# Fetch two pairs ahead, fillers thinned, the last store on another queue: a fused attention and token-routing kernel

## The chip, the cores and the metric

The kernel runs on one NeuronCore of a Trainium2 chip. The core has a matmul engine (PE; weight loads are listed apart as PEld), a vector engine (DVE), a scalar engine (ACT), GpSimd (POOL), SyncE (SP), which here only issues transfers, and 16 DMA engines. Time is device microseconds of one execution; the kernel before takes 159.84 us, median of 3 runs (159.52 to 160.04). A span is the part of it that the profile covers.

## The reference

Two parts follow each other. Attention in chunks of 32 queries: each sees 56 keys (16 to the left, its own 32, 8 to the right) and 8 memory keys. Then a routed FFN: per batch the 128 best of 768 tokens by a gate score get an FFN added.

```python
for c in range(768 // 32):                  # batch 4, 8 heads, head_dim 64
    k_full = concat(mem_k, k[max(0, 32*c-16) : min(768, 32*c+40)])
    a = softmax(q[32*c : 32*c+32] @ k_full.T / 8)
    out[32*c : 32*c+32] = a @ v_full
x = out as [4, 768, 512]                    # heads side by side
scores = x @ w_gate                         # [4, 768]
for b in range(4):
    top = argpartition(-scores[b], 128)[:128]
    xe = x[b, top]
    ye = relu(xe @ w1) @ w2                 # 512 -> 1024 -> 512
    out[b, top] = xe + sigmoid(scores[b, top])[:, None] * ye
```

## The kernel before

Work goes in 16 pairs of heads, n = 0 to 15, four to a batch. Everything is written out in program order for each engine; nothing reorders it later. One turn of the main loop (L537) handles three pairs at once: scores of pair n+1, values of pair n, transposes of pair n+2. It has eight places: scores n+1 first half, q transposes, values n first half ("value half n,0"), k transposes, scores second half, back transposes of the windowed v (vw to vc), value half n,1, v transposes. Between them `hook(i)` calls the steps of the routed FFN that a table puts there (L474 to L500): step i of batch b runs at place i mod 8 of pair 4(b+1) + i div 8. So batch b's routing and FFN run beside the attention of the batches after it; those of batch 2 end, and those of batch 3 run, behind the loop (L576 to L599).

The steps are: six dots with the gate vector on DVE (`m_dot`), transposes that put the scores in a row (`m_row`), a sigmoid (`m_gate_exp`, `m_gate`), six comparisons of all pairs of scores (`m_cmp`) whose matmul counts give each token's rank (`m_count`), a mask and a slot number (`m_mask`, `m_slot`), one-hot selections (`m_sel`), index and gate by a matmul with them and then the indirect DMA that fetches the chosen rows from the output in DRAM (`m_aux` and `m_fetch`, L406), transposes of these rows (`m_rows`, L413), two halves of the first FFN layer (`m_ffn1`), and the second layer with a scatter that adds to the output (`m_ffn2`). Batch 3 does not fetch: it gathers from SBUF by matmuls (`m_gather`).

Transfers go out on two queues. GpSimd issues all loads (converting fp32 to fp16), the fetches and the scatters; SyncE issues the gate vector and the stores of x (`m_store`, two transfers a batch). Loads go by units of two pairs with four buffers, so a unit is issued when the one four before it has been used. Fillers (`fill`, `fill_into`) are matmuls of zeros whose result nobody reads. PSUM pools that the fillers use: pmm (one bank, all routing steps), pxx (one bank, values), pss (two banks, scores and batch 3).

Of the kernel before, what the change touches and what calls it, by code (L numbers as in the profile page):

```python
# [8 lines left out]
FP = mybir.dt.float32  # L9
# [8 lines left out]
def _dap(x, offset, dims):  # L18
    return bass.AP(tensor=x.tensor, offset=offset, ap=[list(d) for d in dims])
# [7 lines left out]
def kernel(  # L27
# [13 lines left out]
    nc = tc.nc  # L41
    B, H, S, D = q.shape
    n_mem = mem_k.shape[2]
    cap = int(moe_capacity)
    Dm = H * D
# [5 lines left out]
    NB = 6  # L51
# [11 lines left out]
    pxx = ctx.enter_context(tc.tile_pool(name="pxx", bufs=1, space=bass.MemoryType.PSUM))  # L63
# [50 lines left out]
    def fill_into(ap, n=1):  # L114
        for _ in range(n):
            nc.tensor.matmul(out=ap, lhsT=zeros[:, 0:128], rhs=zeros, start=True, stop=True)  # L116

    def fill(n):
        fill_into(pmm.tile([128, 1, 512], FP, tag="pm", name="p_f")[:, 0, :], n)

    p_t = ptt.tile([128, 8, 100], F16, tag="tp", name="p_t")
    pads = p_t.bitcast(FP)
# [90 lines left out]
    def tr_q(n):  # L213
        if n >= NPR:
            return
        p_q = pvv.tile([128, 8, 128], F16, tag="pv", name="p_q")[:, :, 0:96]
        transposes(q16s, n, p_q)
        qT = att.tile([128, 96, 8], F16, tag="qT", name="qT")
        nc.scalar.copy(out=qT, in_=p_q.rearrange("p j t -> p t j"))  # L219
        qTs[n] = qT  # L220

    def mem_cols(t, src, n):
        eng = nc.vector if n < 4 else nc.gpsimd
        eng.tensor_copy(out=t.rearrange("p g (j t) -> p g j t", t=16)[:, :, :, 15],  # L224
                              in_=src[:, :, n].unsqueeze(1).to_broadcast([128, NG, n_mem]))

    def tr_k(n):
        if n >= NPR:
            return
        transposes(k16s, n)  # L230
        kw = kws[n % SLOTS]
        nc.vector.tensor_copy(out=kw.rearrange("p g (j t) -> p g j t", t=16),  # L232
                              in_=_sap(p_t, 0, [[12, NG], [100, 8], [1, 16]]))
        if n:
            mem_cols(kw, memkT, n)
# [20 lines left out]
    def scores(n, half, fills=0):  # L256
        if n >= NPR:
            return
        kw, qT = kws[n % SLOTS], qTs[n]
        qf = qT.rearrange("p t j -> p (t j)")  # L260
        p_s = pss.tile([128, 2, 512], FP, tag="ps", name="p_s")
        fill_into(p_s[:, 0, :], fills)
        for gi, g in enumerate(GROUPS[half]):
            for h in range(2):
                o = 64 * h
                nc.tensor.matmul(out=p_s[:, h, 96 * gi:96 * gi + 96], lhsT=kw[o:o + 64, g, :],  # L266
                                 rhs=qf[o:o + 64, 96 * g:96 * g + 96], start=True, stop=True)
        es = att.tile([128, 2, 4, 96], F16, tag="es", name="es")
        pv = p_s[:, :, 0:384].rearrange("p s (g t) -> p s g t", t=96)
        for c in range(3):  # L270
            nc.scalar.activation(out=es[:, :, :, 32 * c:32 * c + 32], in_=pv[:, :, :, 32 * c:32 * c + 32],  # L271
                                 func=AF.Exp, bias=maskb[:, c:c + 1], scale=0.125)
        ess[n, half] = es
# [40 lines left out]

    def m_store(b):
        x = xs[b]
        nc.sync.dma_start(out=_dap(out, b * S * Dm, [[Dm, 96], [96 * Dm, NB], [1, Dm]]), in_=x[0:96, :, :])
        nc.sync.dma_start(out=_dap(out, (b * S + 576) * Dm, [[Dm, 32], [32 * Dm, NB], [1, Dm]]), in_=x[96:128, :, :])

    def m_alloc(b):  # L320
        m = mods[b]
# [145 lines left out]
    def moe_steps(b):  # L467

        st = {}

        def at(i, f, *a):
            st.setdefault(i, []).append(lambda: f(b, *a))

        at(0, m_alloc)  # L474
        p = dict(dots=(0, 3, 6, 7, 8, 11), row0=12, row1=15, gate=17, cmps=(18, 19, 22, 23, 24, 27),
                 counts=(22, 23, 26, 27, 28, 31), mask=32, slot=34, sel=35, fetch=38, rows=45, ffn=(47, 49, 51))
        if b == LAST - 2:
            p.update(fetch=37, rows=43, ffn=(45, 46, 47))
        if b == LAST - 1:
            p = dict(dots=(0, 1, 3, 4, 6, 7), row0=9, row1=11, gate=12, cmps=(13, 14, 15, 17, 18, 19),  # L480
                     counts=(16, 17, 18, 20, 21, 22), mask=22, slot=24, sel=24, fetch=26)
        for i in range(NB):
            at(p["dots"][i], m_dot, (i,))
        at(p["row0"], m_row, 0, 4)
        at(p["row1"], m_row, 4, 6)
        at(p["row1"], m_gate_exp)
        at(p["gate"], m_gate)
        for i in range(NB):
            at(p["cmps"][i], m_cmp, (i,))
        for i in range(NB):  # L490
            at(p["counts"][i], m_count, (i,))
        at(p["mask"], m_mask)
        at(p["slot"], m_slot)
        at(p["sel"], m_sel)
        at(p["fetch"], m_fetch)
        if b < LAST - 1:
            at(p["rows"], m_rows)
            at(p["ffn"][0], m_ffn1, 0)
            at(p["ffn"][1], m_ffn1, 1)
            at(p["ffn"][2], m_ffn2)  # L500
        return st
# [8 lines left out]
        for f in places.get(i, ()):  # L510
            f()

    fill(8)
    tr_k(0)
    fill(2)
    tr_q(0)
# [1 line left out]
    mem_cols(kws[0], memkT, 0)  # L518
    fill(2)
    tr_v(0)  # L520
    fill(1)
    scores(0, 0)
    mem_rows(memv16, memvT)
    for n in range(3):
        mem_cols(vws[n], memvT, n)
    tr_k(1)
    fill(2)
    scores(0, 1)
    tr_q(1)
    fill(2)  # L530
    back_v(0)
    tr_v(1)
    fill(1)
    late_constants()
    scrA = mod.tile([128, NB], FP, tag="scrA", name="scrA")
    scrB = mod.tile([128, NB], FP, tag="scrB", name="scrB")
    for n in range(NPR):  # L537
        b, pr = divmod(n, NP)
        i = 8 * n
        nf = 1  # L540
        if b >= 1 and pr == 0:
            m_store(b - 1)
        if n == 1:
            nc.sync.dma_start(out=wgb, in_=_dap(moe_w_gate, 0, [[0, 128], [1, Dm]]))
        if n == NPR - 2:
            m_alloc(LAST)
        scores(n + 1, 0, nf if b == 0 else 0)
        hook(i)
        if n == NPR - 1:
            m_dot(LAST, range(NB), 0, 2, scrA)  # L550
        if 3 <= n + 3 < NPR:
            mem_cols(vws[(n + 3) % SLOTS], memvT, n + 3)
        tr_q(n + 2)
        hook(i + 1)
        values(n, 0, nf)
        hook(i + 2)
        tr_k(n + 2)
        hook(i + 3)
        scores(n + 1, 1, nf)
        if n == NPR - 2:  # L560
            m_x16(LAST, 0, NB, 0, 2)
        hook(i + 4)
        back_v(n + 1)
        hook(i + 5)
        values(n, 1, nf)
        hook(i + 6)
        tr_v(n + 2)
        hook(i + 7)
        if n % 2 == 1 and n // 2 + 4 < NPR // 2:
            load_unit(n // 2 + 4)  # L570
        if n in (0, 2, 4, 6):
            load_w(n)
            load_w(n + 1)
# [3 lines left out]
    m_store(b)  # L577
    m_dot(b, range(NB), 2, 4, scrB)
    nc.vector.tensor_tensor(out=mods[b].scr, in0=scrA, in1=scrB, op=ALU.add)
    m_rows(b - 1)  # L580
    m_ffn1(b - 1, 0)
    m_ffn1(b - 1, 1)
    m_row(b, 0, 4)
    m_gate_exp(b)
    m_row(b, 4, 6, "dve")
    m_cmp(b, range(NB))
    m_ffn2(b - 1)
    m_x16(b, 0, 6, 2, 4)
# [46 lines left out]
```

## Time and profile before

| what | us |
|---|---|
| median of the runs | 159.84 |
| profiled execution | 159.29 |
| its span | 157.6 |
| PE, DVE, ACT, POOL busy | 119.6, 87.8, 80.9, 49.3 |
| mean granted PE clock | 0.851 of 2.4 GHz |
| DVE busy in 96 to 104 us | 7.64 of 8 |
| scatter, issue to landing, median | 4.7 |
| last count matmuls of batch 3 end | 141.7 |
| last scatter issued | 150.45 |

Read it by stages. The main loop runs from about 18 to 120 us and the rest is the tail, where the routed FFN of batches 2 and 3 stands alone. Up to about 72 us the DMA engines are never free. A clock of 1.00 means 2.4 GHz granted to PE, 0.50 means 1.2 GHz; a stretch between shows that it changed within it.

### The profile page before, as it was taken

What the parts mean: (1) busy time and instruction counts of PE and PEld (TensorE: products, weight loads), DVE (VectorE), ACT (ScalarE), POOL (GpSimd) and SP (SyncE); (2) the same over time, 40 slices, a digit from 0 to 9 for tenths busy, and PEclk for the clock granted to TensorE, in tenths of its full rate; (3) what the DMA queues carried; (4) which work ended last, traced back from release to release, by engine and by line L of the source; (5) the groups of instructions that cost most, each with busy time, mean ns of one, the idle gap of its engine ahead of it and who ended that gap; (6) DMA issues with size and microseconds to landing.
All of it is one profiled execution on the core that took longest, in us unless ns stands there. A gap on an engine that the chain in (4) does not pass through costs nothing. (4 is left out here: it accounts for less than half of the span.)

```text
span 157.6 us, 4751 instructions
## 1 busy us (share of the span) xinstructions
PE 119.6 (76%) x2036; PEld 87.3 (55%) x2036; DVE 87.8 (56%) x280; ACT 80.9 (51%) x159; POOL 49.3 (31%) x82
## 2 busy tenths in 40 slices
PE   6789999999999999901989999949875006877900
PEld 2344677778777787601866876828553005845500
DVE  4425276557997999930116799939189700086000
ACT  3146478888889676810372869556660002451310
POOL 6984543036743671520001621210310200031030
PEclk9955699999999999985559999999998555599975
DMA  3999999999999999994000218520050590004022
GB/s 73 169 165 184 204 208 204 209 206 210 249 288 253 207 205 234 292 262 67 0 4 0 44 29 228 179 33 0 4 69 0 148 269 19 0 0 67 4 28 38
DMA packets 15781, 19.90 MB, mean 126 GB/s; under 512 B 848, under 2 KB 11536, under 8 KB 15760
## 3 DMA queue, kind: packets, MB, share of 16 engines
q0 software_dynamic: 12416, 13.04, 51.4%
q1 hardware_dynamic: 3344, 6.55, 13.5%
q8 instruction: 16, 0.26, 0.6%
q14 instruction: 5, 0.04, 0.1%
HBM read 24.25 MB, written 7.34 MB: 200 GB/s over the span
## 5 line engine op out<-in xcount | busy, mean ns | idle before, releaser
L271 ACT ACTIVATE es<-p_s,maskb 128x256 f16<-128x256 f32 x96 | 38.5, 475 | 6.6 <-PE p_s L266 6.5
L292 PEld LDWEIGHTS <-es 128*32 128x32 f16 (+1 forms) x384 | 21.7, 112 | 4.5 <-issue 0.2
L292 PE MATMUL p_w<-vc,es 128*32 128x65 f16 (+1 forms) x384 | 23.0, 203 | 0.0
L242 ACT COPY vw<-p_t 128x960 f16<-128x960 f16 x16 | 15.4, 961 | 14.5 <-PE p_t L210 13.0
L224 POOL COPY kw<-memkT 128x64 f16<-128x64 f16 x12 | 8.0, 664 | 45.2 <-DVE kw L232 45.2
L295 DVE RECIPROCAL rd<-p_w 128x6 f32<-128x6 f32 x32 | 6.1, 192 | 22.5 <-PE p_w L292 22.0
L296 DVE TENSOR_TENSOR x<-p_w,rd 128x384 f32<-128x384 f32 x32 | 17.8, 558 | 1.1
L464 POOL DMA_INDIRECT out_dram<-y,idx x4 | 6.7, 1668 | 34.6 <-ACT y L463 34.6
L417 PE MATMUL p_e<-ident,xe 128*128 128x128 f16 x12 | 1.6, 278 | 19.3 <-DMA xe<-out_dram,idx 19.3
L333 DVE SCALAR_TENSOR_TENSOR junk<-x,wgb 128x512 f32<-128x512 f32 (+1 forms) x30 | 16.2, 584 | 0.0
L219 ACT COPY qT<-p_q 128x768 f16<-128x768 f16 x16 | 13.0, 814 | 5.1 <-PE p_q L210 5.1
L371 DVE TENSOR_SCALAR gr<-brow,scr 128x768 f16<-128x768 f32 x24 | 14.1, 631 | 0.1
L251 DVE COPY vc<-p_v 128x1024 f16<-128x1024 f16 x16 | 11.0, 687 | 4.4 <-PE p_v L250 4.3
L419 ACT COPY xeT<-p_e 128x512 f16<-128x512 f16 x3 | 1.8, 585 | 22.5 <-PE p_e L417 22.5
L116 PE MATMUL p_w<-zeros 128*128 128x512 f16 x32 | 12.5, 391 | 0.2 <-DVE idx L439 0.2
L417 PEld LDWEIGHTS <-xe 128*128 128x128 f16 x12 | 0.9, 120 | 19.7 <-DMA xe<-out_dram,idx 19.7
L451 PEld LDWEIGHTS <-w_sb 128*128 128x128 f16 x128 | 10.4, 122 | 2.6 <-issue 1.7
L232 DVE COPY kw<-p_t 128x1024 f16<-128x1024 f16 x16 | 10.9, 683 | 1.4 <-PE p_t L210 1.4
L266 PE MATMUL p_s<-qT,kw 64*128 64x96 f16 x256 | 11.6, 212 | 0.0
L266 PEld LDWEIGHTS <-kw 64*128 64x128 f16 x256 | 6.7, 97 | 7.7 <-issue 6.6
L116 PE MATMUL p_f<-zeros 128*128 128x512 f16 x21 | 9.3, 563 | 2.0 <-DVE zeros L110 1.3
L250 PE MATMUL p_v<-ident,vw 128*128 128x128 f16 x128 | 10.2, 225 | 0.6 <-ACT qT L219 0.6
(111 smaller groups left out, 200.4 us busy)
## 6 DMA issues: line engine op xcount, KB each, us to landing
out_dram<-x SPq DMA_DIRECT2D x4, 1152.0 KB, 9.1
k<-in_k_dram POOLq DMA_DIRECT2D x7, 384.0 KB, 11.7
q<-in_q_dram POOLq DMA_DIRECT2D x7, 384.0 KB, 13.1
v<-in_v_dram POOLq DMA_DIRECT2D x7, 384.0 KB, 14.5
w_sb<-in_moe_w_dram POOLq DMA_DIRECT2D x8, 256.0 KB, 11.9
out_dram<-x SPq DMA_DIRECT2D x4, 384.0 KB, 10.4
k<-in_k_dram POOLq DMA_DIRECT2D x2, 192.0 KB, 4.7
q<-in_q_dram POOLq DMA_DIRECT2D x2, 192.0 KB, 4.9
```

The costliest lines, as they stand in the source:

```text
L116: nc.tensor.matmul(out=ap, lhsT=zeros[:, 0:128], rhs=zeros, start=True, stop=True)
L219: nc.scalar.copy(out=qT, in_=p_q.rearrange("p j t -> p t j"))
L232: nc.vector.tensor_copy(out=kw.rearrange("p g (j t) -> p g j t", t=16), in_=_sap(p_t, 0, [[12, NG], [100, 8], [1, 16]]))
L242: nc.scalar.copy(out=vw.rearrange("p g (j t) -> p g j t", t=16)[:, :, :, 0:15], in_=_sap(p_t, 0, [[12, NG], [100, 8], [1, 15]]))
L251: nc.vector.tensor_copy(out=vcs[n % SLOTS][:, :, :, 0:64], in_=p_v)
L266: nc.tensor.matmul(out=p_s[:, h, 96 * gi:96 * gi + 96], lhsT=kw[o:o + 64, g, :], rhs=qf[o:o + 64, 96 * g:96 * g + 96], start=True, stop=True)
L271: nc.scalar.activation(out=es[:, :, :, 32 * c:32 * c + 32], in_=pv[:, :, :, 32 * c:32 * c + 32], func=AF.Exp, bias=maskb[:, c:c + 1], scal ...
L292: nc.tensor.matmul(out=p_x[r0:r1, i, h, :], lhsT=es[:, h, gi, q0:q1], rhs=vc[:, GROUPS[half][gi], h, 0:65], start=True, stop=True)
L296: nc.vector.tensor_tensor(out=xs[b].rearrange("p g (n h d) -> p n g h d", n=NP, d=D)[:, pr, 3 * half:3 * half + 3], in0=p_x[:, :, :, 0:64] ...
L333: nc.vector.scalar_tensor_tensor(out=junk[:, c0:c1], in0=x[:, bl, c0:c1], scalar=1.0, in1=wgb[:, c0:c1], op0=ALU.mult, op1=ALU.mult, accum ...
L371: nc.vector.tensor_scalar(out=m.gr[:, bl, :], in0=m.brow, scalar1=m.scr[:, bl:bl + 1], scalar2=None, op0=ALU.is_lt)
L451: nc.tensor.matmul(out=p_h[:, 0, 128 * fi:128 * fi + 128], lhsT=w1_sb[:, dch, f0:f0 + 128], rhs=m.xeT[:, dch, :], start=(dch == 0), stop=( ...
```

## The change

Four things differ. The table of steps: for batches 0 and 1 the rows and the FFN come later behind the fetch, the six counts stand together, and the row transposes one step later; for batch 2 the slot, the selection and the fetch share one step, at the start of pair 15. Behind the loop the score row of batch 3 comes ahead of batch 2's first FFN layer, with eight fillers ahead of both. The store of x for the last batch is issued by GpSimd. Fillers: one or two per pair (none ahead of scores any more), more in the prologue, and in the bank of pool pxx instead of pmm; in the prologue the q transposes of pair 1 move ahead of its k transposes.

```diff
@@ fill
-        fill_into(pmm.tile([128, 1, 512], FP, tag="pm", name="p_f")[:, 0, :], n)
+        fill_into(pxx.tile([128, 512], FP, tag="px", name="p_f"), n)
@@ m_store
-        nc.sync.dma_start(out=..., in_=x[0:96, :, :])
-        nc.sync.dma_start(out=..., in_=x[96:128, :, :])
+        eng = nc.gpsimd if b == LAST else nc.sync
+        eng.dma_start(out=..., in_=x[0:96, :, :])
+        eng.dma_start(out=..., in_=x[96:128, :, :])
@@ moe_steps
-        p = dict(dots=(0, 3, 6, 7, 8, 11), row0=12, row1=15, gate=17, cmps=(18, 19, 22, 23, 24, 27),
-                 counts=(22, 23, 26, 27, 28, 31), mask=32, slot=34, sel=35, fetch=38, rows=45, ffn=(47, 49, 51))
+        p = dict(dots=(0, 3, 6, 7, 8, 11), row0=13, row1=16, gate=17, cmps=(18, 19, 22, 23, 24, 27),
+                 counts=(30, 30, 30, 31, 31, 31), mask=31, slot=34, sel=35, fetch=37, rows=54, ffn=(55, 57, 59))
         if b == LAST - 2:
-            p.update(fetch=37, rows=43, ffn=(45, 46, 47))
+            p.update(rows=46, ffn=(47, 48, 50))
         if b == LAST - 1:
...
-                     counts=(16, 17, 18, 20, 21, 22), mask=22, slot=24, sel=24, fetch=26)
+                     counts=(21, 21, 21, 22, 22, 22), mask=22, slot=24, sel=24, fetch=24)
@@ main loop
-        nf = 1
+        nf = 0 if b == 0 or n in (10, 11, 13, 14) else 1
-        scores(n + 1, 0, nf if b == 0 else 0)
+        scores(n + 1, 0)
-        scores(n + 1, 1, nf)
+        scores(n + 1, 1)
-        values(n, 1, nf)
+        values(n, 1, 1)
@@ behind the loop
+    fill(8)
     m_rows(b - 1)
-    m_ffn1(b - 1, 0)
-    m_ffn1(b - 1, 1)
     m_row(b, 0, 4)
     m_gate_exp(b)
     m_row(b, 4, 6, "dve")
+    m_ffn1(b - 1, 0)
+    m_ffn1(b - 1, 1)
     m_cmp(b, range(NB))
```

The first place is ACT around batch 0's rows, whose copy is xeT<-p_e; brow is batch 1's score row, hT and y the FFN of batch 0, es, qT and vw the attention. Before:

```order
L350 COPY brow<-p_m 128x512
L419 COPY xeT<-p_e 128x512
L242 COPY vw_166<-p_t 128x64x15
L453 ACTIVATE hT<-p_m 128x512
L350 COPY brow<-p_m 128x256
L355 ACTIVATE gt<-scr 128x6
L271 ACTIVATE es<-p_s,maskb 128x8x32 x3
L219 COPY qT<-p_q 128x768
L453 ACTIVATE hT<-p_m 128x512
L463 ACTIVATE y<-p_m,gate 128x512
```

And of the changed kernel:

```order
L352 COPY brow<-p_m 128x512
L242 COPY vw_166<-p_t 128x64x15
L271 ACTIVATE es<-p_s,maskb 128x8x32 x3
L352 COPY brow<-p_m 128x256
L357 ACTIVATE gt<-scr 128x6
L219 COPY qT<-p_q 128x768
L271 ACTIVATE es<-p_s,maskb 128x8x32 x3
L421 COPY xeT<-p_e 128x512
L242 COPY vw_154<-p_t 128x64x15
L455 ACTIVATE hT<-p_m 128x512
```

The rows moved from ahead of vw_166 to ahead of vw_154, a pair and a step later, behind both copies of batch 1's score row.

The second place is DVE in pair 15: sel, idx and gate are batch 2's selection, index and gate, x the output of the last pair, junk,scrA and junk,scrB the two halves of batch 3's dots. Before:

```order
L403 TENSOR_SCALAR sel<-iota_171,slot 128x128 x6
L333 SCALAR_TENSOR_TENSOR junk,scrA<-x_2238,wgb 128x256 x6
L295 RECIPROCAL rd<-p_w 128x6
L296 TENSOR_TENSOR x_2238<-p_w,rd 128x3x128
L439 TENSOR_SCALAR idx<-p_m 128x1
L441 TENSOR_REDUCE gate<-p_m 128x1
```

And of the changed kernel:

```order
L405 TENSOR_SCALAR sel<-iota_171,slot 128x128 x6
L441 TENSOR_SCALAR idx<-p_m 128x1
L443 TENSOR_REDUCE gate<-p_m 128x1
L335 SCALAR_TENSOR_TENSOR junk,scrA<-x_2223,wgb 128x256 x6
L295 RECIPROCAL rd<-p_w 128x6
L296 TENSOR_TENSOR x_2223<-p_w,rd 128x3x128
```

The index, for which the fetch waits, moved ahead of six dots and one value half.

The third place is the end of GpSimd's order, before and then changed: xe is batch 2's fetch, y the scatters of batches 1 to 3, x the last store.

```order
L464 DMA out_dram<-y,idx 1536x512
L410 DMA xe<-out_dram,idx 128x512
L464 DMA out_dram<-y,idx 2304x512
L464 DMA out_dram<-y,idx 3072x512
L630 UNCONDITIONAL_BRANCH
```

```order
L466 DMA out_dram<-y,idx 1536x512
L412 DMA xe<-out_dram,idx 128x512
L319 DMA out_dram<-x_2223 96x6x512
L320 DMA out_dram<-x_2223 32x6x512
L466 DMA out_dram<-y,idx 2304x512
L466 DMA out_dram<-y,idx 3072x512
```

The store stands behind batch 2's fetch and ahead of the last two scatters.

## Rows read from the trace of the kernel before

**Rows 1.** Stretches: from:to, length, busy us of each engine, PEclk, DMA share, GB/s.

```profile
19.00:36.00 17.00, 17.00 (x361) 12.83 (x356) 10.12 (x23) 14.03 (x30) 5.42 (x11) 1.00 1.23 207
...
52.00:66.00 14.00, 13.63 (x307) 10.67 (x302) 13.37 (x42) 10.76 (x22) 7.34 (x12) 1.00 1.21 232
...
66.80:74.40 7.60, 0.03 (x1) 0.00 (x0) 1.51 (x4) 0.78 (x2) 1.12 (x2) 0.68 0.84 177
...
74.40:82.90 8.50, 7.79 (x89) 6.44 (x90) 1.47 (x6) 4.51 (x9) 0.00 (x0) 0.50 0.01 2
...
104.00:112.00 8.00, 6.86 (x94) 4.82 (x96) 4.18 (x11) 4.31 (x9) 0.26 (x1) 1.00 0.01 2
...
120.30:130.50 10.20, 0.00 (x0) 0.00 (x0) 4.71 (x25) 0.00 (x0) 0.99 (x1) 0.52 0.62 166
...
130.50:138.00 7.50, 6.13 (x45) 5.34 (x46) 0.42 (x1) 2.47 (x5) 0.00 (x0) 0.51 0.01 4
```

**Rows 2.** Waits: who waited for whom, total us, times, longest.

```profile
PE p_e L417 <- DMA xe<-out_dram,idx: 19.3, 3, 10.3
```

**Rows 3.** Timeline: start, length, engine, line, operation; GpSimd's last load and batch 0's fetch.

```profile
58.14 0.68 POOL L83 DMA_DIRECT2D v<-in_v_dram  x1
...
64.10 1.30 POOL L410 DMA_INDIRECT xe<-out_dram,idx  x1 [2.79 <-DVE gate L441]
```

**Rows 4.** DMA issues of 56, 63, 100, 122 us: count, KB, us to landing.

```profile
v<-in_v_dram POOLq DMA_DIRECT2D x1, 384.0 KB, 15.6
...
xe<-out_dram,idx POOLq DMA_INDIRECT x1, 10.3
...
xe<-out_dram,idx POOLq DMA_INDIRECT x1, 3.5
...
out_dram<-x SPq DMA_DIRECT2D x1, 384.0 KB, 8.0
...
xe<-out_dram,idx POOLq DMA_INDIRECT x1, 8.1
```

**Rows 5.** Timeline of pairs 1 and 2: fillers (L116) and what follows them.

```profile
20.55 0.39 PE L116 MATMUL p_s<-zeros 128*128 128x512 f16 x1
...
20.87 0.20 PEld L266 LDWEIGHTS <-kw 64*128 64x128 f16 x8 [0.23 <-issue]
...
23.98 0.39 PE L116 MATMUL p_w<-zeros 128*128 128x512 f16 x1
...
24.21 0.71 PE L292 MATMUL p_w<-vc,es 128*96 128x65 f16 x12
...
28.74 0.39 PE L116 MATMUL p_w<-zeros 128*128 128x512 f16 x1
```

**Rows 6.** Timeline of PE, pairs 10 to 13, [idle before <-releaser].

```profile
84.49 1.90 PE L460 MATMUL p_m<-w_sb,hT 128*128 128x512 f16 x8
...
87.48 0.71 PE L292 MATMUL p_w<-vc,es 128*96 128x65 f16 x12
...
92.95 0.71 PE L292 MATMUL p_w<-vc,es 128*96 128x65 f16 x12
...
104.25 0.40 PE L417 MATMUL p_e<-ident,xe 128*128 128x128 f16 x4 [1.46 <-DMA xe<-out_dram,idx]
```

**Rows 7.** Timeline of pair 15 and the tail, PE and DVE.

```profile
117.69 0.18 PE L394 MATMUL p_m<-incl,ltri 128*128 128x1 f16 x1 [0.92 <-DVE incl L389]
...
118.17 1.07 DVE L403 TENSOR_SCALAR sel<-iota,slot 128x128 f16<-128x128 f16 x6
...
121.93 0.15 DVE L439 TENSOR_SCALAR idx<-p_m 128x1 int32<-128x1 f32 x1
...
124.94 0.17 DVE L579 TENSOR_TENSOR scr<-scrA,scrB 128x6 f32<-128x6 f32 x1
...
131.79 1.87 PE L451 MATMUL p_m<-xeT,w_sb 128*128 128x128 f16 x16 [0.67 <-ACT xeT L419]
...
136.00 1.49 PE L344 MATMUL p_l<-ident,scr 128*128 128x128 f32 x6
```

More of the change, by code (lines that the diff above doesn't have):

```diff
@@ L316, in m_store @@
         x = xs[b]
-        nc.sync.dma_start(out=_dap(out, b * S * Dm, [[Dm, 96], [96 * Dm, NB], [1, Dm]]), in_=x[0:96, :, :])
-        nc.sync.dma_start(out=_dap(out, (b * S + 576) * Dm, [[Dm, 32], [32 * Dm, NB], [1, Dm]]), in_=x[96:128, :, :])
+        eng = nc.gpsimd if b == LAST else nc.sync
+        eng.dma_start(out=_dap(out, b * S * Dm, [[Dm, 96], [96 * Dm, NB], [1, Dm]]), in_=x[0:96, :, :])
+        eng.dma_start(out=_dap(out, (b * S + 576) * Dm, [[Dm, 32], [32 * Dm, NB], [1, Dm]]), in_=x[96:128, :, :])
     def m_alloc(b):
@@ L511, in hook @@
             f()
-    fill(8)
+    fill(12)
     tr_k(0)
@@ L520 @@
     tr_v(0)
-    fill(1)
+    fill(3)
     scores(0, 0)
@@ L525 @@
         mem_cols(vws[n], memvT, n)
+    tr_q(1)
+    fill(2)
     tr_k(1)
-    fill(2)
     scores(0, 1)
-    tr_q(1)
     fill(2)
@@ L532 @@
     tr_v(1)
-    fill(1)
+    fill(2)
     late_constants()
```

## The prediction, made before the changed kernel ran

> **What bounds the kernel now.** I read the stretches first (busy time of each engine beside the granted clock), then the waits, the timeline at both ends of each long wait, and last the DMA issues. The chain of waits is of no use here: it breaks off after a few microseconds of unexplained issue time, so the bound is read stage by stage. In pairs 0 to 3 TensorE (PE) is busy throughout (19 to 36 us, [rows 1]). Then PE stands still twice with little running beside it: 66.8 to 74.4 us and 120.3 to 130.5 us. Both times it waits for rows fetched by the indirect DMA; these two waits and a third, short one make 19.3 us [rows 2]. Each long wait is paid twice, because the granted clock falls to 0.50 during it (1.2 of 2.4 GHz) and stays there some 8 us into the work that follows: 74.4 to 82.9 and 130.5 to 138 us [rows 1].
>
> The two fetches are late for different reasons. That of batch 0 is issued at 64.10 and takes 10.3 us [rows 3, 4]. It is queued on the GpSimd DMA queue behind the loads: the last of them, v of the final unit, is issued at 58.14 and takes 15.6 us, so it lands at 73.7, and the rows come 0.7 us after it. The DMA engines are full from 19 us on (share over 1 in rows 1), so the load stream itself sets that moment. The fetch of batch 1, with nothing beside it, takes 3.5 us. That of batch 2 takes 8.1 us, because the 1.5 MB store of x3 starts 0.5 us after it and lands with it, its second part 8.0 us after issue [rows 4].
>
> The end is a chain: score row of batch 3 (transposes on PE), six comparisons on VectorE (DVE), counts, slots, gather, FFN, scatter. It can't start before 136.0, though the scores of rows 7 are ready at 125.1, since in PE's order the transposes stand behind the batch 2 rows and its whole first FFN layer [rows 7].
>
> **The change, part by part.** Times are of the profiled execution: span 157.6, its own time 159.29, so 1.69 lies around the span; the median 159.84 is 0.55 above it.
>
> *Everything before pair 10 (prologue, fillers of batch 0 and 1).* A filler ahead of a value product costs 0.23 us (start of the filler to start of the product), one ahead of scores 0.32 (to the first weight load) [rows 5]. Batch 0 loses 0.32 + 0.23 + 0.32 = 0.87 us of PE work per pair. A pair takes 4.76 now (23.98 to 28.74, [rows 5]), so PE would need 3.9; ScalarE has 14.03 us in 17 us of pairs [rows 1], also 3.9 per pair. I take 4.2, so 4 x 0.55 = 2.2 us. From pair 7 on DVE is nearly full (13.37 of 14 us [rows 1]), so 0 to 1.5 us there. The prologue is not shown in its new order; the reordering and the fillers that no longer wait for PSUM give between nothing and 3.5 us (the PE stretch from 8.4 to 18.5 us, mostly at the lower clock, could shrink by a third). In all PE runs 2 to 7 us ahead.
>
> I count all of this at nothing. PE now meets the batch 0 rows after value half 10,1 instead of before 9,1. From 66.8 that is 5.6 to 6 us of steps later, about 72.6; less 2 to 7 us it is 65.6 to 70.6. The rows land when the load stream has ended, and that moves the same bytes through the same full engines. Without the lag of a store issued among them I take 73.3, with 71.5 (DMA share falling from 71 us on) and 74.4 (as before) as bounds. So a stall of 3 to 8 us remains, and whatever is saved ahead of it turns into waiting. In the wait from 66.8 to 74.4 the granted clock is 0.68 on the mean and 0.50 at the end, so I take it as fallen again.
>
> *Pairs 10 and 11, after the stall.* The stretch from 74.4 to 82.9 carried rows, a filler, a value half, v transposes, two FFN halves with a 0.69 us bank wait, two score-row transposes, scores and q transposes. Behind the new place PE has the same list with one k transpose (0.78 from start to start at this clock) for the filler, the row transposes and the bank wait: 8.0 us. Then second FFN layer, scores, vw transposes, filler, value half, which took from 84.49 to 87.48 + 0.71 = 88.2 [rows 6], less a score filler: 3.4. So value half 11,1 ends at 73.3 + 8.0 + 3.4 = 84.7; before it was 93.6 (92.95 + 0.71 = 93.66, [rows 6]). Gain 8.9. If the clock did not fall, 3 us more; if the bunched counts wait for comparisons, 1 us less.
>
> *Pairs 12 to 15.* Before, 93.6 to 120.3, 26.7 us. The wait of 1.46 us for batch 1's rows goes (three steps later, fetch 3.5 us), and so does the 0.68 us that the row transposes wait behind them (at 105.3, [rows 6] for the rows themselves). Five fillers less are 1.4 us, of which half counts, as DVE has little room beside the steps of these pairs (7.64 of 8 us from 96 to 104). What is late next is the pair 15: slot, selection and index product now stand ahead of both value halves. PE waits from 117.69 until the selection, which starts on DVE at 118.17 and takes 1.07, has been multiplied; value half 15,1 ends about 1.0 us later relative to the slot product [rows 7]. Sum 26.7 - 1.46 - 0.68 - 0.7 + 1.0 = 24.9; bounds 23 and 29, since the moved FFN halves could meet DVE work instead. End of the values: 109.6.
>
> *Batch 2's fetch and the end.* The index now comes before the six half dots, not after them and a value half: 121.93 becomes about 119.6 in the old clock of the program [rows 7]. The store of x3 follows it on the same queue and only when x3 is complete, 3 us later. I take 3.5 us to landing (bounds 3.5 and 8.1; the nearest row without a store is batch 1's). In the program it waits for batch 1's scatter too, which by the steps between is issued some 5.5 us ahead and lands in 4.7 (page, median); up to 1 us late costs nothing, since the eight fillers and the scores come later still. On DVE nothing disappears, so the scores are ready 5.0 us after the last value half, as now (124.94 + 0.17 against 120.26). Then row transposes 1.1 and two FFN halves: 1.87 each at 1.2 GHz [rows 7], so 1.0 at 2.4, with the 0.67 that PE waits before each [rows 7] once between them and once behind; second layer 1.9 [rows 6], counts 1.1: 7.5 us. The comparisons, 3.3 us on DVE, lie beside the FFN. Counts end 12.5 after the values at the higher clock, and 2.3 later at the lower one (two FFN halves, and the transposes half as long again). PE has idle time of up to 2.8 us between fillers and scores, so either may happen; I take the middle, 13.6. Before it was 141.7 - 120.3 = 21.4. From there the chain is unchanged: 157.6 - 141.7 = 15.9. End of the span: 109.6 + 13.6 + 15.9 = 139.1; with 1.69 around it 140.8, about **141** (the median's 0.5 is within the rounding of the terms).
>
> The store's issue on GpSimd is not shown. Its bounds are 0.3 us (SP's own issue) and 2 us (loads of 384 KB take 0.68 each to issue); landing between 8 us (as on SP) and 15.6 (a load in a full queue). Queued behind it are the scatters of batches 2 and 3 alone. Issued near 113, it lands between 121 and 130, and the last scatter is issued near 132: cost 0. With a later landing the end moves one to one.
>
> The Trainium skill, "DMA: Bandwidth & Descriptors", section "Issuing engine by pattern", speaks against this edit: plain stores belong on Sync, whose path is generally the faster one. Here the rows only say that a store on SP doubles the time of a fetch beside it; by the rule the store would be last to land, which is the third rival.
>
> **The rivals.**
> 1. *No stall, or too short for the clock to fall.* For it: if DVE holds pairs 5 to 10 and the prologue gives nothing, PE arrives near 71, only 2 us before the landing. Against: 4 us of fillers and waits are gone. The stretch after the stall then loses its surcharge of 3 us for the lower clock, and with the higher clock in the tail 1.1 more: 137.
> 2. *A new wait in pairs 12 to 15 and the lower clock in the tail:* 29 instead of 24.9, and 1.2: 146. For it: DVE in these pairs.
> 3. *The store on the GpSimd queue ends last.* Landing 4 us after the last scatter could start: 145. Against: some 2 us of slack even at 15.6 us.
> 4. *Slower: the fillers held the clock.* Without them PE falls to 1.2 GHz in the pairs themselves. Steps spaced as at the lower clock (scores 0.43 twice, q, k and v transposes 0.78 each, values 1.04 twice, vw 0.94, a filler 0.43) make 6.7 us per pair against 4.76, so 2.0 more. The gain of 19 and the 5 us of slack ahead of the landing are used up from twelve pairs on; with all sixteen and the FFNs low it is about 175. Against: from 104 to 112 us PE was busy 6.86 of 8 us, less than these pairs will be, and the clock stayed at 1.00 [rows 1].
> The Trainium skill, "TensorE: Matmul & The Clock Gate", section "HAM oscillation — how this bites in real kernels", says that PE left waiting for DMA is throttled again and restarts cold. Both long waits here agree (granted 0.50 after each); for the pairs it would matter only if the waits within them sufficed, and the row just named speaks against that.
> 5. *It does nothing:* the rows of batch 0 are met at their landing as before, and 2's fetch still takes 8 us. The former alone leaves the tail's 8 us; both together are hardly possible, as the row transposes no longer wait for the FFN.
>
> **How the numbers follow.** Forecast 141 with 47%, its own range 138.5 to 143.5; rival 1 22%; rival 2 16%; rival 3 8%; rival 4 4%; rival 5 or still less gain 3%. Holding 8 in 10 takes 134 to 148: the bounds above summed are -1.8 - 3 - 2 - 1.2 and +1.1 + 1 + 4 + 1.2, and these don't all fall together. A difference of 0.3% is about what this kernel's runs can tell from none. Faster 0.95 (all but rival 4 and part of 5), same 0.01, slower 0.04.
>
> **What would show it.** Rows of batch 0 start on PE between 71.5 and 74.4, after a wait of 3 to 8 us, with the clock at 0.50 behind it; batch 1's wait gone; batch 2's fetch lands within 4 us and PE's wait for it is under 2 us; score transposes start near 114.5, not 136; pairs of batch 0 near 4.2 us. I am wrong if the rows of batch 0 land well before 71 us (the loads were not the limit), if the granted clock in pairs 0 to 9 falls, or if the last scatter waits for the store.

## The result, and the profile after

The changed kernel takes 139.58 us (median of 4 runs, 138.15 to 140.1) against 159.84 us for the kernel before on the same chip: ratio 0.872 (95% interval 0.863 to 0.881). The forecast was 141, range 134 to 148. Some executions of a kernel are over 1.5% longer than its fastest, mostly at a lower granted clock; ratios and times below leave them out unless a clock is named beside them.

| what | before | after |
|---|---|---|
| profiled execution, us | 159.29 | 139.08 |
| its span | 157.6 | 137.4 |
| PE, DVE, ACT, POOL busy | 119.6, 87.8, 80.9, 49.3 | 111.7, 87.5, 80.0, 50.5 |
| mean granted PE clock | 0.851 | 0.936 |
| last count matmuls of batch 3 end | 141.7 | 121.3 |
| last scatter issued | 150.45 | 130.04 |

PE is busy 8 us less, in part because the same work runs at the higher clock, DVE and ACT are busy as long as before, and 20 us are gone: the waits and the slow stretches behind them. First the waits of PE (who waited for whom, total us, times, longest). The line that answers to [rows 2], PE for the fetched rows with 19.3 us, is no longer among the first:

```profile
PE p_v L250 <- ACT qT L219: 4.3, 7, 0.7
PE p_q L210 <- DMA q<-in_q_dram: 2.5, 2, 1.7
```

In place of the long waits stand many short ones. The timeline of PE (start, length, engine, line, operation, [idle before <-releaser]; L419 transposes the fetched rows, L116 the fillers, L292 the value halves, L396 the slot product, L438 the index products, L453 and L462 the FFN, L346 the score row, L383 the counts):

```profile
17.53 0.53 PE L210 MATMUL p_q<-ident,q 96*64 96x96 f16 x16 [1.71 <-DMA q<-in_q_dram]
...
35.94 0.39 PE L116 MATMUL p_w<-zeros 128*128 128x512 f16 x1
...
60.50 0.18 PE L438 MATMUL p_m<-aux,sel 128*128 128x3 f16 x1 [0.39 <-DVE sel L405]
60.91 0.67 PE L438 MATMUL p_m<-aux,sel 128*128 128x3 f16 x5 [0.23 <-DVE sel L405]
...
64.64 0.61 PE L116 MATMUL p_w<-zeros 128*128 128x512 f16 x1
...
75.07 0.40 PE L419 MATMUL p_e<-ident,xe 128*128 128x128 f16 x4
...
82.93 0.71 PE L292 MATMUL p_w<-vc,es 128*96 128x65 f16 x12
...
94.23 0.43 PE L346 MATMUL p_m<-ident,scr 128*128 128x128 f32 x2 [0.82 <-ACT brow L352]
...
106.40 0.18 PE L396 MATMUL p_m<-incl,ltri 128*128 128x1 f16 x1 [0.86 <-DVE incl L391]
107.20 1.00 PE L438 MATMUL p_m<-aux,sel 128*128 128x3 f16 x6 [0.62 <-DVE sel L405]
...
109.88 1.11 PE L292 MATMUL p_w<-vc,es 128*96 128x65 f16 x12
110.92 2.86 PE L116 MATMUL p_f<-zeros 128*128 128x512 f16 x8
113.61 0.39 PE L419 MATMUL p_e<-ident,xe 128*128 128x128 f16 x4
114.34 0.84 PE L346 MATMUL p_l<-ident,scr 128*128 128x128 f32 x6 [0.34 <-DVE scr L581]
115.02 1.06 PE L453 MATMUL p_m<-xeT,w_sb 128*128 128x128 f16 x16
...
120.25 1.04 PE L383 MATMUL p_l<-onec,gr 128*128 128x1 f16 x36
```

The rows of batches 0 and 2 (75.07, 113.61) start without a wait, the weight load for those of batch 1 after one of 0.27 us, and the score transposes of batch 3 start at 114.34 instead of 136.00 [rows 7]. The first FFN half of batch 2 takes 1.06 us instead of 1.87. On DVE, batch 2's selection and batch 3's scores, whose rows of before are in [rows 7]:

```profile
106.89 1.07 DVE L405 TENSOR_SCALAR sel<-iota,slot 128x128 f16<-128x128 f16 x6
...
114.03 0.17 DVE L581 TENSOR_TENSOR scr<-scrA,scrB 128x6 f32<-128x6 f32 x1
```

GpSimd's own timeline (fetches L412, store L319, last scatter L466), and the landing of batch 0's fetch and of the store's two parts (KB, us from issue):

```profile
62.89 1.06 POOL L412 DMA_INDIRECT xe<-out_dram,idx  x1 [2.10 <-PE p_w L292]
...
109.31 1.04 POOL L412 DMA_INDIRECT xe<-out_dram,idx  x1 [3.85 <-DVE junk L335]
112.23 0.83 POOL L319 DMA_DIRECT2D out_dram<-x  x1 [1.87 <-DVE x L296]
...
130.04 1.57 POOL L466 DMA_INDIRECT out_dram<-y,idx  x1 [6.97 <-ACT y L465]
```

```profile
xe<-out_dram,idx POOLq DMA_INDIRECT x1, 11.6
...
out_dram<-x POOLq DMA_DIRECT2D x1, 1152.0 KB, 6.8
out_dram<-x POOLq DMA_DIRECT2D x1, 384.0 KB, 7.3
```

Batch 0's fetch lands at 62.9 + 11.6 = 74.5, as late as before (64.10 + 10.3 = 74.4, [rows 3, 4]); PE arrives 0.6 us behind it instead of 7.6 ahead. The store lands near 120, 10 us ahead of the last scatter. The stretches (columns as in [rows 1]):

```profile
8.00:16.00 8.00, 7.08 (x153) 4.17 (x147) 4.15 (x17) 5.92 (x11) 4.66 (x8) 1.00 1.16 178
16.00:20.00 4.00, 2.47 (x61) 2.15 (x62) 1.19 (x3) 2.39 (x7) 2.76 (x10) 1.00 1.24 206
...
62.00:66.00 4.00, 4.00 (x63) 3.15 (x61) 3.35 (x11) 2.47 (x5) 1.56 (x2) 0.50 1.13 290
...
75.00:83.70 8.70, 8.27 (x151) 6.27 (x148) 6.25 (x14) 5.94 (x12) 2.48 (x4) 1.00 0.01 3
...
106.00:112.00 6.00, 4.99 (x36) 3.20 (x37) 5.30 (x29) 0.01 (x1) 1.04 (x1) 0.50 0.51 58
...
114.00:121.30 7.30, 5.58 (x83) 4.34 (x84) 3.85 (x8) 3.35 (x7) 0.00 (x0) 1.00 0.69 199
```

The clock is 2.4 GHz behind batch 0's rows (75 to 83.7) and in the tail from 114, where it was 1.2 GHz before [rows 1]. It still falls twice, from about 61.5 to 68.5 and from 106 to 113: the first time behind waits for a selection (L438, 0.39 and 0.23 us), the second within a wait of 0.86 us for the slots (L396). Waits of 0.38 and 0.23 us for batch 1's selection (at 88.58 and 88.98 us) leave it at 1.00.

### The profile page after: what moved, and what is told of

Same layout as the page of the kernel before. It is cut to its first block, busy times and chain, and to the rows that moved or that the text cites. A ratio compares the mean times of both kernels' runs of the same rounds, so it can differ in the third digit from the quotient of the medians.

```text
span 137.4 us, 4727 instructions
## 1 busy us (share of the span) xinstructions
PE 111.7 (81%) x2024; PEld 83.0 (60%) x2024; DVE 87.5 (64%) x280; ACT 80.0 (58%) x159; POOL 50.5 (37%) x84
## 4 chain that ended last, share of the span: by engine, by line
PE 31%; DVE 15%; ACT 14%; issue 14%; DMA 14%; POOL 6%; POOLq 1%
ACT es L271 7%; DMA q<-in_q_dram 7%; PE p_w L292 7%; PE p_t L210 5%; PE p_v L250 4%; DMA xe<-out_dram,idx 3%; DMA out_dram<-y,idx 3%; DVE junk L335 3%; DVE x L296 3%; ACT qT L219 3%; PE p_w L116 3%; PE p_m L462 3%; PE p_m L453 2%; DVE gr L373 2%; PE p_m L383 2%
## 5 line engine op out<-in xcount | busy, mean ns | idle before, releaser
L292 PEld LDWEIGHTS <-es 128*32 128x32 f16 (+1 forms) x384 | 22.1, 116 | 4.4 <-issue 0.7
L292 PE MATMUL p_w<-vc,es 128*32 128x65 f16 (+1 forms) x384 | 24.4, 208 | 0.0
L466 POOL DMA_INDIRECT out_dram<-y,idx x4 | 6.5, 1635 | 24.7 <-ACT y L465 23.4
L295 DVE RECIPROCAL rd<-p_w 128x6 f32<-128x6 f32 x32 | 6.1, 191 | 12.5 <-PE p_w L292 12.1
L116 PE MATMUL p_f<-zeros 128*128 128x512 f16 x36 | 12.8, 496 | 1.3 <-DVE zeros L110 1.3
L250 PEld LDWEIGHTS <-vw 128*128 128x128 f16 x128 | 8.1, 100 | 5.6 <-issue 4.1
L116 PEld LDWEIGHTS <-zeros 128*128 128x128 f16 x60 | 5.9, 110 | 8.9 <-issue 4.6
L210 PE MATMUL p_q<-ident,q 96*64 96x96 f16 x256 | 8.8, 213 | 2.6 <-DMA q<-in_q_dram 2.5
L116 PE MATMUL p_w<-zeros 128*128 128x512 f16 x24 | 9.8, 410 | 1.0 <-DVE x L296 1.0
L210 PEld LDWEIGHTS <-q 96*64 96x64 f16 x256 | 6.7, 113 | 4.5 <-DMA q<-in_q_dram 2.7
L453 PEld LDWEIGHTS <-w_sb 128*128 128x128 f16 x128 | 7.6, 97 | 2.5 <-issue 1.6
## 6 DMA issues: line engine op xcount, KB each, us to landing
out_dram<-x SPq DMA_DIRECT2D x3, 1152.0 KB, 11.5
```

The lines of the kernel that those rows point to most:

```text
L210: nc.tensor.transpose(out=dst[64 * h:64 * h + 64, j, :], in_=src[n][:, h, 64 * j:64 * j + 64], identity=ident16[0:96, 0:96])
L250: nc.tensor.transpose(out=p_v[:, g, :, :], in_=vws[n % SLOTS][:, g, :], identity=ident16)
L292: nc.tensor.matmul(out=p_x[r0:r1, i, h, :], lhsT=es[:, h, gi, q0:q1], rhs=vc[:, GROUPS[half][gi], h, 0:65], start=True, stop=True)
```

## The experiments

All edits are made to the changed kernel, and one not told stays as it was changed.

### Rows of batch 0 at their old place

```diff
-... rows=54, ffn=(55, 57, 59))
+... rows=45, ffn=(47, 49, 51))
```

> The changed kernel with batch 0's rows and FFN at their old places (step 45, FFN 47, 49, 51); everything else as changed. Theory (the load stream sets the landing of batch 0's fetch at about 74.5 us, whatever PE does): PE meets the rows near 67 us, waits 6 to 8 us until 74.5, the clock falls, and the time is 144 to 148. Rival (the rows would have been there by then, since PE runs ahead only a little and the fetch is issued a step earlier): no wait over 2 us, 139 to 141.

149.4 us (148.67 to 149.51), ratio 0.944 (0.936 to 0.952): 9.8 us above the changed kernel (11.5 by the difference of the two ratios), a little more than expected. The row transposes in its timeline:

```profile
74.14 0.61 PE L419 MATMUL p_e<-ident,xe 128*128 128x128 f16 x4 [7.75 <-DMA xe<-out_dram,idx]
```

The wait of 7.75 us is back, with the landing where it was (fetch issued 63.0, landed 11.1 us later), and the granted clock was 0.66 in 74 to 82. About half of the whole gain is this one move, rows and FFN together.

### The same, with the last unit of loads left out

This kernel is the one above without the loads of the last unit; pairs 14 and 15 are computed from the q, k and v of pairs 6 and 7.

```diff
-if n % 2 == 1 and n // 2 + 4 < NPR // 2:
+if n % 2 == 1 and n // 2 + 4 < NPR // 2 - 1:
```

> The kernel e1_rows_early without the last load unit: pairs 14 and 15 are computed from the q, k and v of pairs 6 and 7, so 1.2 MB of 9.4 MB of loads are left out. Theory (the load stream, at some 205 GB/s, sets the landing of the fetch behind it): landing 5 to 6 us earlier, near 68.5, PE's wait of 7.8 us shrinks to 1 to 3, time 140 to 144. Rival (the fetch itself takes 10 us, whatever is queued ahead): landing within 1.5 us of 74, time as e1, 148 to 150.

144.59 us (one run). Batch 0's fetch, by its DMA issue:

```profile
xe<-out_dram,idx POOLq DMA_INDIRECT x1, 4.6
```

Issued at 63.74, it lands in 4.6 us instead of 11.1, and the rows start at 69.18 without a wait; PE came there later than in the kernel above (69.2 against 66.4), with its clock at 0.50 from 60 to 72 us. So it is the loads queued ahead of the fetch that set its landing, not the fetch or its index. The kernels that keep all loads say the same: issued anywhere from 62.76 to 67.86 us, the fetch landed between 74.1 and 75.1, each time within 0.7 us of the last load. Whether the order in the queue or the full DMA engines hold it back was not separated.

### The old fillers in the loop

```diff
-nf = 0 if b == 0 or n in (10, 11, 13, 14) else 1
+nf = 1
-scores(n + 1, 0)
+scores(n + 1, 0, nf if b == 0 else 0)
-scores(n + 1, 1)
+scores(n + 1, 1, nf)
```

> The changed kernel with all fillers of the loop as before (four per pair in batch 0, three after). Theory (in batch 0 PE now waits 0.7 us per pair for ScalarE's copy of q, where the fillers stood): pairs of batch 0 take 4.7 to 4.8 us against 4.67, and the time is within 0.7 us of the changed kernel, or up to 2 us lower if the fillers hold the clock at 61 us. Rival (a filler costs its 0.23 or 0.32 us of PE everywhere): pairs of batch 0 at 5.4, time 143 or more.

138.99 us (138.4 to 140.33, 6 runs), ratio 0.877 (0.872 to 0.882): the same. A filler of two pairs in its timeline, and then the vw transposes of two pairs in the changed kernel's:

```profile
27.40 0.39 PE L116 MATMUL p_w<-zeros 128*128 128x512 f16 x1
...
32.16 0.39 PE L116 MATMUL p_w<-zeros 128*128 128x512 f16 x1
```

```profile
28.77 0.61 PE L250 MATMUL p_v<-ident,vw 128*128 128x128 f16 x8 [0.70 <-ACT qT L219]
...
33.44 0.61 PE L250 MATMUL p_v<-ident,vw 128*128 128x128 f16 x8 [0.69 <-ACT qT L219]
```

A pair takes 4.76 us with the fillers and 4.67 without: the place of the two fillers is taken by a wait of 0.70 us for ACT's copy of q. With them the mean clock was 0.955 instead of 0.936, and the rows of batch 0 even waited 0.84 us, until 74.44.

### q of four pairs copied by DVE

```diff
-nc.scalar.copy(out=qT, in_=p_q...)
+if 2 <= n <= 5:
+    nc.vector.tensor_copy(out=qT, in_=p_q...)
+else:
+    nc.scalar.copy(out=qT, in_=p_q...)
```

> The changed kernel with q of pairs 2 to 5 copied by VectorE instead of ScalarE, so that in batch 0 the copy no longer stands behind the exponentials. Theory (the 0.7 us per pair that PE now waits for that copy is what became of the removed fillers; but what is gained ahead of 74.5 us is lost waiting for batch 0's rows): pairs of batch 0 take 4.0 to 4.3 us instead of 4.67, a wait of 0.5 to 2 us appears at the rows, and the time is 138 to 139.7. Rival (early gains count in full): 136.5 to 137.5. Rival (PE work, not the copy, sets the pair): pairs stay at 4.6 or more.

139.98 us (139.38 to 140.52), ratio 0.879 (0.873 to 0.886). In its timeline:

```profile
27.05 0.38 PE L116 MATMUL p_w<-zeros 128*128 128x512 f16 x1
...
31.01 0.38 PE L116 MATMUL p_w<-zeros 128*128 128x512 f16 x1
```

The pairs now take 4.0 us, so ACT's copy was what held them. But the rows start at 75.10 all the same, just behind the fetch (issued 64.95, landing 10.1), and the wait of 0.5 to 2 us that was expected there is not seen. PE had lost the gain before: the waits for q's own loads grow from 2.5 to 4.2 us in all, and the clock was 0.50 from 18 to 24 us, where the changed kernel had 1.00. So this run shows what set the pairs, and not what becomes of time that is won ahead of the landing.

### Work ahead of pair 0: order and fillers

Three kernels. The first has the old order and the old numbers of fillers; the second the new order with the old numbers; the third the old order with the new numbers.

```diff
 # old numbers (first and second kernel)
-fill(12); tr_k(0) ... fill(3); scores(0, 0) ... tr_v(1); fill(2)
+fill(8);  tr_k(0) ... fill(1); scores(0, 0) ... tr_v(1); fill(1)
 # old order (first and third)
-tr_q(1); fill(2); tr_k(1); scores(0, 1)
+tr_k(1); fill(2); scores(0, 1); tr_q(1)
```

> The work ahead of pair 0 in its old order and with the old number of fillers (8, 2, 2, 1, 2, 2, 1), the rest as changed. Theory (nothing that is won ahead of the batch 0 rows counts, as VectorE in pairs 6 to 9 and the landing of the fetch at 74.4 set them): rows of batch 0 within 0.7 us of 75.1, time 138.5-140.5. Rival (the prologue's gain reaches the rows): value half of pair 0 starts 1 us or more later than 18.0, and so do the rows, 76 or later; time 140.5-142.

140.64 and 141.07 us (the other two executions 144.16 and 145.04, both at a clock of 0.917), where the kernel before took 157.67 to 159.63 beside it. A stretch and the rows in its profile (span 139.4):

```profile
16.00:20.00 4.00, 3.53 (x57) 2.48 (x54) 0.92 (x7) 2.97 (x5) 2.61 (x9) 0.50 1.24 205
```

```profile
77.58 0.40 PE L419 MATMUL p_e<-ident,xe 128*128 128x128 f16 x4
```

The theory fell in this execution. The clock falls near 13 us, within a wait of 1.39 us for q, and is still at 0.50 here; PE is 2.5 us later by pair 8, the rows start at 77.58 instead of 75.07, and the end is 2.0 us later. So time lost ahead of pair 0 can reach the end. Whether the old order and numbers lost it is another matter, as the runs below show.

> Order of the work ahead of pair 0 as changed (q transposes of pair 1 ahead of its k transposes), numbers of fillers as before the change (8, 2, 2, 1, 2, 2, 1); the loop as changed. With the old order and the old numbers the clock fell at 13 us and the rows of batch 0 started at 77.6 instead of 75.1. Theory (the fillers do it: TensorE waits for the loads in any order, and with fewer fillers these waits let the clock fall): granted clock 0.5 to 0.6 from about 12 to 20 us, first value half after 18.5, rows at 76.5-78, time 140-142.5. Rival (the order does it): clock 1.00 throughout, first value half near 18.0, rows near 75, time 138.5-140.3.

144.08 to 145.92 us, ratio 0.912 (0.900 to 0.923): slower than theory and rival had it. In the profiled execution (clock 0.731) the granted clock was 0.75 to 0.85 even in the pairs, which no other showed, so I read only its start, where PE waits 2.04 us for q until 11.78:

```profile
12.00:16.00 4.00, 4.00 (x48) 2.23 (x45) 0.99 (x2) 1.94 (x4) 1.43 (x3) 0.50 1.22 198
```

> Numbers of fillers as changed (12, 2, 2, 3, 2, 2, 2), order of the work ahead of pair 0 as before the change. Theory (the fillers do it): granted clock 1.00 up to 20 us, first value half within 0.5 us of 18.0, rows of batch 0 within 0.7 of 75.1, time 138.5-140.5. Rival (the order does it): clock down near 13 us, rows at 76.5-78, time 140-142.5.

139.59 and 140.65 us, ratio 0.880 (0.868 to 0.893). In the profiled execution (143.11, clock 0.899; another took 143.4 at 0.883):

```profile
12.00:16.00 4.00, 3.08 (x60) 1.86 (x60) 2.34 (x10) 2.53 (x5) 1.34 (x2) 1.00 1.22 198
16.00:20.00 4.00, 2.08 (x40) 1.67 (x34) 0.00 (x0) 2.23 (x5) 2.45 (x9) 0.66 1.24 205
```

```profile
18.05 0.85 PE L210 MATMUL p_q<-ident,q 96*64 96x96 f16 x16 [1.92 <-DMA q<-in_q_dram]
```

In these three executions the clock is down from 12 or 13 us on with the old numbers, in either order, and with the new ones it stands until the wait at 16 us. That does not settle it. The nine other kernels of this section all have the changed order and numbers ahead of pair 0, and in the profiled executions of five of them the clock fell there too: on the mean of 12 to 16 us it was 0.50 to 0.68, among them the one with fillers where the clock falls (0.57), which at 140.09 us is level with the changed kernel. The one without the eight fillers:

```profile
12.00:16.00 4.00, 3.83 (x45) 2.07 (x46) 0.99 (x2) 1.56 (x4) 1.34 (x2) 0.50 1.23 202
```

In the other four and in the changed kernel it stayed at 1.00. The same instructions keep the clock in one execution and lose it in another, so one execution of each kernel can't show what the order or the numbers do to it; nor can these say whether the clock survives the wait at 16 us (1.71 us at 1.00 in the changed kernel, 1.92 us and a fall here). The times don't decide it either: with the old order the numbers make no difference beyond the spread (140.64 and 141.07 against 139.59 and 140.65), with the new order the old numbers are 4 to 8 us slower, and why stays open.

### Batch 2's fetch at its old place

```diff
-mask=22, slot=24, sel=24, fetch=24)
+mask=22, slot=24, sel=24, fetch=26)
 # and the store by SP:
-eng = nc.gpsimd if b == LAST else nc.sync
+eng = nc.sync
```

> The changed kernel with batch 2's fetch two steps later, as before, and the last store on SyncE, as before. Theory (late index and the store beside the fetch make it land about 8 us after issue, and the row transposes of batch 3 stand behind these rows): fetch issued near 111.5, landing after 118, PE waits 5 to 8 us, time 144 to 148. Rival (the new order behind the loop already hides the fetch): PE waits under 3 us, 139 to 141.5.

144.37 us at a clock of 0.928, 147.95 in the profiled execution at 0.879, and 150.94 and 151.26 at 0.859 and 0.847. The row transposes:

```profile
120.27 0.61 PE L419 MATMUL p_e<-ident,xe 128*128 128x128 f16 x4 [6.18 <-DMA xe<-out_dram,idx]
```

As expected: issued at 112.08 beside the store it takes 8.1 us again, and PE waits 6.18. Two things are back at once here, the place of the fetch and the queue of the store; the next kernel has the queue alone.

### The last store on SP

```diff
-eng = nc.gpsimd if b == LAST else nc.sync
+eng = nc.sync
```

> The changed kernel with the last store of x back on SyncE's queue. Theory (the fetch is issued 3 us ahead of the store and has landed before the store moves): no difference, 139 to 140.2, rows of batch 2 on PE without a wait over 0.5 us. Rival (queue matters: on two queues the store takes turns with the fetch): the rows come up to 4 us later, 141 to 143.

139.19, 141.77, 143.19 and 144.29 us at clocks of 0.951, 0.897, 0.893 and 0.873: the first is level with the changed kernel, and the times give no verdict beyond that. The profiled run (139.19) shows the landings:

```profile
out_dram<-x SPq DMA_DIRECT2D x1, 1152.0 KB, 6.3
...
xe<-out_dram,idx POOLq DMA_INDIRECT x1, 3.5
```

The fetch takes 3.5 us with the store on SP, so its earlier place freed it, not the queue of the store. The store lands as on GpSimd.

Up to the last store this kernel is the changed one, and still batch 0's rows went otherwise in this execution:

```profile
PE p_e L419 <- DMA xe<-out_dram,idx: 1.6, 1, 1.6
```

The clock held at 61 us without any edit there, PE came to the rows at 72.8 and waited until 74.44, and the clock fell behind that wait (0.57 in 76 to 80). Value half 11,1 ended at 84.21 instead of 83.64, and the counts at 121.42 instead of 121.29: this stall cost next to nothing.

### The tail: old order without fillers, and the fillers alone

```diff
 # first kernel
-fill(8); m_rows(b - 1); m_row(b, 0, 4); m_gate_exp(b); m_row(b, 4, 6, "dve"); m_ffn1(b - 1, 0); m_ffn1(b - 1, 1)
+m_rows(b - 1); m_ffn1(b - 1, 0); m_ffn1(b - 1, 1); m_row(b, 0, 4); m_gate_exp(b); m_row(b, 4, 6, "dve")
 # second kernel
-fill(8)
```

> The changed kernel with the old order behind the loop: no eight fillers, batch 2's first FFN layer ahead of batch 3's row transposes. Theory (the order is worth two FFN halves, as the transposes stand on the path that ends last): row transposes start near 118 us instead of 114.3, counts end near 124, time 142 to 143.5. Rival (the early landing of the rows was all; PE has to do the FFN before the counts in either order): at most 0.7 us over the changed kernel, 139 to 140.3.

143.68 us at a clock of 0.891 (the profiled execution) to 150.24 at 0.828, too uneven for a ratio. In the profile:

```profile
113.05 0.61 PE L419 MATMUL p_e<-ident,xe 128*128 128x128 f16 x4 [2.27 <-DMA xe<-out_dram,idx]
```

The score transposes start at 118.23, behind both FFN halves, and the counts end at 123.24, as the theory had them: 12.5 us after the values instead of 10.3. Behind them the clock falls again (0.56 in 124 to 130).

> The eight fillers ahead of batch 2's rows are left out, everything else stays. Theory (they only fill time in which TensorE would wait for the scores anyway, but they also bring the clock back, which was 0.50 at 106.5-113 us and 1.00 from 113): the rows start when the fetch has landed, near 112.8-113.6, transposes of the scores still near 114.3 as VectorE sets them; the clock stays at 0.50 into the first FFN layer, so the two halves take 1.87 instead of 1.05 and the counts end 1.5 to 2.5 us later: span 138.5-140, time 140-142. Rival A (the comparisons on VectorE set the end of the counts): within 0.7 us of the changed kernel, 139-140. Rival B (the fillers themselves are in the way): faster, 137-138.5, with the transposes ahead of 113.5.

142.82 to 144.24 us, ratio 0.908 (0.897 to 0.918): slower than every theory had it. The tail of the profiled execution (148.03, clock 0.832, batch 0's rows 6 us late already, though up to there the code is the changed kernel's):

```profile
119.10 0.61 PE L419 MATMUL p_e<-ident,xe 128*128 128x128 f16 x4 [2.02 <-DMA xe<-out_dram,idx]
120.43 1.51 PE L346 MATMUL p_l<-ident,scr 128*128 128x128 f32 x6 [0.72 <-DVE scr L581]
121.74 1.91 PE L453 MATMUL p_m<-xeT,w_sb 128*128 128x128 f16 x16
```

The score transposes start 3.4 us after the values, as with the fillers, so these delay nothing. Without them the transposes and the first FFN half run at 1.2 GHz (1.51 and 1.91 instead of 0.84 and 1.06), and the counts end 11.8 us after the values instead of 10.3. The rest of the difference to the changed kernel, 2 to 3 us, is not explained by that.

### Fillers where the clock falls

Two fillers ahead of batch 0's index product, and four and three around batch 2's slot and index products.

```diff
+ fill(2)    # m_fetch, b == 0
+ hold(4)    # m_slot,  b == LAST - 1
+ hold(3)    # m_fetch, b == LAST - 1
```

> The changed kernel with fillers where PE waits for the selection: two ahead of batch 0's index product (pair 8), four ahead of batch 2's slot product and three ahead of its index product (pair 15). Theory (the clock falls at 61 and 106 us because PE idles there, and only the second costs, since up to 74.5 us PE is ahead of the fetch anyway): clock 1.00 in pairs 9 and 15, rows of batch 0 wait up to 2 us for a landing at 74 to 74.5, time 137.5 to 139. Rival (both falls cost their lower-clock work): 135.5 to 137. Rival (fillers don't hold it): 139 to 140.5.

139.96 us (139.18 to 140.09; a fourth took 142.08 at a clock of 0.924), ratio 0.878 (0.869 to 0.887): no gain. A stretch and batch 0's rows:

```profile
56.00:72.00 16.00, 14.32 (x314) 11.36 (x315) 13.06 (x45) 12.56 (x27) 5.42 (x9) 1.00 1.16 244
```

```profile
74.38 0.61 PE L428 MATMUL p_e<-ident,xe 128*128 128x128 f16 x4 [1.57 <-DMA xe<-out_dram,idx]
```

The clock holds through both places (1.00 also in 104 to 122). That the fillers hold it is not shown: at 61 us it also held in four kernels without them, and past the two waits at 106 in two (the one with q copied by DVE, until 110, and the one with the old work ahead of pair 0). With the clock held, PE reaches the rows at 72.8 and waits for the landing, and there the clock falls after all (0.60 in 72 to 80). In the tail the value halves end at 110.86, about as before, and the score transposes wait until 115.35 for DVE.

## Why the prediction was right, and where it wasn't

The sum of the prediction against the profile, in us:

| term | predicted | measured |
|---|---|---|
| batch 0's rows start | 73.3 | 75.1 |
| from there to the end of value half 11,1 | 8.0 + 3.4 | 83.64 - 75.07 = 8.6 |
| pairs 12 to 15 | 24.9 | 110.99 - 83.64 = 27.3 |
| end of the values to end of the counts | 13.6 | 121.29 - 110.99 = 10.3 |
| the rest | 15.9 | 16.1 |
| span | 139.1 | 137.4 |

*Right.* The landing of batch 0's fetch: as late as before with every version that keeps the loads, and 6 us earlier without their last unit. Batch 1's wait is down from 1.46 to 0.27 us, though its fetch took 4.8 us and not 3.5. Batch 2's fetch, issued at 109.31, is there when PE comes to the rows at 113.61, and the score transposes start at 114.34 (114.5 was said). The store on GpSimd costs nothing. Fillers of the loop count for nothing. The last stretch is unchanged.

*Wrong: "In all PE runs 2 to 7 us ahead"*, and with it the stall of 3 to 8 us and "I count all of this at nothing". PE was to reach batch 0's rows at 65.6 to 70.6; it came at 75.07, just behind the landing, and nothing stalled. In the other executions that are profiled with the same code up to there (four) it came between 72.8 and 81.4, and only the earliest of them waited, 1.65 us. Two things ate the lead. In the pairs of batch 0 the fillers were not on the path alone: ACT's copy of q stood right behind them, so a pair went from 4.76 to 4.67, not 4.2. And the 2.0 us of lead at pair 4 (35.94 against 37.94 in the trace of before) was lost by pair 9 (64.64 against 63.81), in pairs in which DVE is nearly full and, from 61.5, at the low clock; where the clock held (the store on SP) that filler started at 63.35. The two fillers in the trace of before:

```profile
37.94 0.39 PE L116 MATMUL p_w<-zeros 128*128 128x512 f16 x1
...
63.81 0.39 PE L116 MATMUL p_w<-zeros 128*128 128x512 f16 x1 [0.17 <-DVE idx L439]
```

Since the landing and PE's arrival are level, each side counts in one direction: a later PE ends later (2.0 us in the execution with the old prologue), an earlier one waits (the store on SP, the old fillers, the held clock: 1.65, 0.84 and 1.57 us). Counting what is won ahead of the rows at nothing was therefore wrong in kind: it counts as far as it brings PE to the landing.

*The clock behind the rows.* With no stall it did not fall, so the 11.4 us became 8.6. That is the first rival's mechanism (no stall "if DVE holds pairs 5 to 10") and its price of 3 us, with an arrival 4 us later than it had. In the execution with the store on SP, where the clock did fall behind the wait of 1.65 us, the same stretch took 84.21 - 74.44 = 9.8. The result lies between the forecast of 141 and that rival's 137.

*Pairs 12 to 15 and the tail were mis-sized by +2.4 and -3.3 us*, and most of that is one error. I measured from the end of the last value half on PE, but in pair 15 DVE sets the pace: from the start of batch 2's selection to the end of batch 3's scores it works almost without a gap, 114.20 - 106.89 = 7.3 us (before 125.11 - 118.17 = 6.9, [rows 7]). The value halves now lie late within this stretch, each at 1.11 instead of 0.71 us, so they end later and the scores follow 3.2 us behind them, not 5.0. From value half 11,1 to the scores it was 30.6 us; 24.9 + 5.0 = 29.9 had been predicted. The second rival's new wait is there (0.82 for a row copy on ACT at 94.23), and costs little. Of the tail's term 1.5 us are left: 7.1 instead of 8.6 from the scores to the counts. There I took the middle of two clocks; the fillers run during the wait for the scores, and the clock is back at 113.

So the total came out by errors that cancel: +1.8 - 2.8 + 2.4 - 3.3 + 0.2 = -1.7. Undone one by one, the edits are worth: the rows of batch 0 about 10 us, batch 2's fetch about 5 (one execution, with the store back on SP), the tail's order and fillers about 2 in the tail itself, the loop fillers and the store's queue nothing that could be measured. For the prologue the executions differ too much to say. No version tried was faster than the changed kernel by more than its own spread.

## What to carry to other kernels

Before moving a consumer away from a late transfer, find out what sets the landing: here it was the queue of loads, so the moved step should aim at that moment, and what is saved ahead of it counts only as long as PE comes later than that. Take a filler's price from what stands right behind it; if another engine's result arrives then, removing the filler makes a wait of the same length. A long wait that goes is worth itself and the slow clock behind it (7.75 us of wait were 9.8 us of time), and fillers that run in a wait that can't be removed are worth the clock they bring back (an FFN half of 1.06 instead of 1.91 us). Before a stretch's clock is put down to an edit, look whether other executions of the same code show it.

## What the runs showed of the chip that I had not expected

The length of a single wait does not tell whether the clock falls. It stayed at 1.00 over a wait of 1.71 us at 16 to 17.5 and fell within one of 0.86 in the same execution (106); over 1.92 us at the former place it fell in another kernel. Nor does the code tell: ahead of pair 0 it fell in five of ten executions of the same instructions. An indirect fetch queued behind loads took 6.8 to 11.6 us to land, the less the later it was issued, and 4.6 without the last of these loads, 3.5 with a store issued well behind it, 8.1 with a store issued beside it. The 1.5 MB store landed after 6.8 and 7.3 us from GpSimd's queue and after 6.3 and 7.3 from SP's.
